# An interleaved long convolution and MLP on one core: another order for the first three quarters of its operations

## The chip, the cores and the metric

The kernel runs on one core of one Trainium2 chip. The metric is the device time of one execution in microseconds (us); the median of three executions stands for a kernel. A profile shows one more execution.

The core has five engines, each of which takes its own instructions strictly in order: TensorE (PE in the profile; its weight loads are PEld), VectorE (DVE), ScalarE (ACT), GpSimd (POOL) and SyncE (SP). They wait for each other and for transfers by semaphores. Here SyncE issues nearly all transfers (DMA), GpSimd a few gathers.

## The reference

With a sequence of 2048 rows and 640 channels, all in float32, the reference computes

```python
x = q
for _ in range(2):
    x = x + A(layernorm(x), k, v)
    x = x + relu(layernorm(x) @ w1) @ w2          # 640 -> 1728 -> 640

def A(q, k, v):                                   # H3 layer
    k_shift = causal_depthwise_conv(k, shift_k)   # 4 taps
    kv = k_shift * v
    y = long_causal_conv(kv, ssm_k) + kv * ssm_D  # 2048 taps per channel, by FFT
    return q * y
```

The convolution doesn't depend on `x`: only its gate, the last product, does. Its result is the same in both rounds, so the kernel computes it once and uses it twice.

## The kernel before, in words

**Tiles.** The sequence is cut into 8 chunks of 256 rows; a chunk has two halves of 128 rows, one per partition. Names carry the chunk: `x2_0` is half 0 of chunk 2's activations, `xT2_1` the transposed, layer-normalised input of chunk 2's second MLP.

**The MLP.** `prep` computes the statistics, normalises (`xnB`), splits the result into two float16 halves (the high one by ScalarE, L1154; the low one by VectorE, L1155) and has SyncE transpose both, for each half chunk, by DMA (L1182) into `xT`: `xT2_1_00` is the high part, `xT2_1_01` the low one. `main` then multiplies: the first product `mm1` (L1319 and L1321 for the first block of columns, where the low part is read last; L1331, L1332, L1334 for the others) into PSUM tiles `h`, of which ScalarE takes the relu's high half `hh` (L1470) and VectorE the rest `hl` (L1471), and the second product `mm2` (L1303, L1304, L1306) into `o` and `oc`, in half blocks of two groups of columns. So `hl10_0` is the low half of the first block of MLP number 10.

**The convolution.** It runs over pairs of channel tiles ("units", named by chunk and tile, `4_2`). `transform` loads `kt` and `vt` (keys and values), `hf` and `hr` (the long filter), applies the four taps (`acc`, on ScalarE L479 and L529 and on VectorE L536 and L553), forms the spectra of the filter (`pg`, L585, with the constants `cG` and `cX`) and, over a transpose `pt` and its eviction `sh` (L651), those of the input (`pr`, L656, with the constant `cM`), evicts them to `gt` and `at` (L670), mirrors them by a GpSimd gather (`at<-at`, L626), and stores them in DRAM (`A`, `G`). `products` loads `Ax` and `Gx` back (L748), multiplies (`pd`, L761), adds up (`pacc`, L766), and transforms back into `u`, `pq` and `ys`, which is stored as `Y`. Each chunk goes through both rounds before the next ones do (a layernorm needs only its own row), so the units of later chunks run beside the MLPs of earlier ones, and after the last unit the MLPs of the last chunks go on alone.

**The order.** The functions above don't issue instructions; they record 4073 operations, with what each reads and writes, in a `Plan`. `table` decodes a constant, `ORDER`, into a permutation of them, and `issue` goes through it once. So `ORDER` alone sets the order of the instructions on every engine's queue, and also in what order buffers of a ring are handed out. Which wait belongs to an instruction follows from what it reads and writes, not from `ORDER`.

```python
    def table(self):
        return [self.ops[k] for k in np.frombuffer(base64.b85decode(ORDER), "<u2")]

    def issue(self):
        for o in self.table():
```

**The start.** TensorE has nothing to multiply yet and runs throwaway matmuls (`spin`, L1579, L1599). ScalarE runs a throwaway square root (`warm`, L1575). SyncE's queue sends the first loads. `kt_0` and `kt_4` share a buffer.

Of the kernel before, what the change touches and what calls it, by code (L numbers as in the profile page):

```python
# [26 lines left out]
C = 256
# [38 lines left out]
    "ssOA2umH3GjsVgC(*U>t*8q<IHvzQ(?f}&QIRV%JCIKh`DglrHECJa7E&=cW+W;^DG66IJI{~%;ya3by)&Sf9+5kNPw*Wr@-2glR"
    "-T>kNJ^?@hHUT&RIsp&?y#NvcNdZd%5djkc;{fac?Epam-vCVk^8ge9PXS5+OaZ<CLIFboL;)2676IS@<^UZ5?*QQd7XkbLMFIT)"
    "{s2({=KxayzW^8kMgdg;=l~f3M*&v>ApsfzSpfk7NCAZb=>Q`ETLB^gZ2@iph5>K^BmwaN@&Jbci2;fMivdmnT>%0CZvg`V1OagY"
    "{{VUc_5h3lUjcFf9szR!Pytc_Q~`DYhyh^%bOBZYSOHoATmfDIcmZGmV*!l;j{#HwjsbT8djVnrkpO)Gd;w$uzX5px<p6#GWdXne"
    "W&wWzkO9E~X91A`k^%GpfC0h*XaQ*f!vVzs#sMG!!~tpnlL3JNlmV3ix&X@o%mK#%_W;NNmjRXmnE}lKf&yy+m;r+U^#IWU>j2UL"  # L70
    "$pHWX$^p{>&H;o0@&TLyngP@Sp8=f#fCBRY^Z^9{g94xd^#P#)_5t_+q5=2;`2n5*_W{oV&;j`XqXDG>qyf7C`T&~&hysBEi2|nq"
    "`T?c^`v9o{r~&)|{Q-sos{#7~2LXoyssYyl+5y-BtO2b7Yylhr*#T7m+X2-99|5HTgaWSt0s`Ryg#xDniUP0!t^w8o-T?*y2m#*#"
    "u>rFIvH=MJ3jrGe-~o#Qv;lPi3IVkN3;_cIi~`&N-2tfr9|NWWf&sSywgKV+xB=w>;{mGz=K<sajslMY*aGMQxdG_`+5)-(lmhAj"
    "4FTo>>jAp~jRNce{sFuJl>)s1tOB|Mw*rs?z5x#bkplk#00IF5?E#kpr~>W*?*Rk?3IdV>m;&$tmI4I=z5)mW@c||RCjuw}ssfV&"
    "1_HSPy8<NwxB{61DFO`wDgp@t2Lj{(ECQSY4gw1T4+5P66aw4=y#l}jtpY6qE&>h#ngTBZt^%F{paKj66#^Clp8~J~5dsndFan_h"
# [5 lines left out]
    "UjkzSV+08UegZ-RU;<?VWCAJ!)&eU7rvx1Xe*$O(W&$h&EdvSz3j;#~Hv}&OFarz&4FfI%L<2<wF#`?*X#{HoJp?}lX97k8K?F|("
    "Q3OH+M+15UXaYb4G6ORMLj*_z9s_IyNdry;s06A6Py{psN&`y+4+CieH3LrrL<B_yPy<E;QUp^3R0CB5Y63O`M+A5THv>2WZ3IXJ"
    "O$1B>ZUj*SRs&4~QUg;1S_4!BIRjk-Nd!s+Is<?NJOfSyR|IbaR|9?o5CeMzSOZxDRRnMZaRgQbUIR-6fdoDSOayWSs{~sEg9L;G"
    "Tmy0fYXW2gd<1g@qy%9DJp*C`Wdm3QUju&xU<0NEK?6GjSp-@Hdjf(4W&?BtV*_~vX9H>jbp);ih6Hv5g#>5=TLfzZTm-NLhXj!X"
    "Km%O_#RRDYhy-i{_ym0fbpw(Fi3F4cb_2%*l?3_(iUi06Z3908lLU_hUIeiOuLNlWZUc7%iv)NBj0Bbh8U=R*%>=9jkObQU`~-~z"
    "js$N5a077ztps@kaszq;djrk{nFPxO%mmN`d;@(0{RDvn&jfP=#srrHngoIag9EYz(*&CYgafk#wgi|2v;@=ye*^ynU<A<wegl95"
    "00p%KbOW3OhXaTM`2>vv(gcYEodk*lw*<HZ{se^skOPqeh69cRo&*C0j{~^`mjlTJp9Iwex&(^@)&%<m0R@x;y9B%hl>?Roj04vM"
    "k^{;Fz68Al*aX}J*#wva-UOWklLK%Co&(<m-~^xqcm=-%zyz5C;RKrlc?FsS+60^f0tKi8p97!+!35m|;soOa<OIS51O=%B!vv}W"
    "1qI~<b_E;-<^*vCA_T4j1_fUPp#ygXuLH0H=LDhz2L<Q^#02UDqXnx2dIft0q64f0+XM&&?gXO)r3HQkas{yiqyu~f2?ewRwF3(U"
    "=>)9<3I(MD>jduveFf|UrUP>Yrv(fJx&ylde+7UAwgU|XrvtJByaT-hvjevS4h6si4+Y!<@C4lh-UHtQs0H8y;sb#N5C!oB@&pkD"  # L90
    "xC3+rss+OX69uaU%>{J@?F9A&qy@wSf(5|?xdW~R!UOXJ;{)UasRa@Rz5~AluLZ{g$OGjA<^vQ3u?5Nlg9XV0=L6^itOe-<#RJR*"
    "^aO_mgayU}rUexRtp)1?&;zms76t4Bi3QOE%LC2>&jZo}%md8>iUo)T7zNY=)dh<M(*xB5?F01$)&tiAvjvO=jRlSc?*r}w@B{G!"
    "@&k_r7X|eLum!aRp#+fy*aP+h)CJiCk_FlWkOhSWBLwpUBm|QMwgvP9B?Kk}v<0^X;RE{v)&=(i_yhR^h6Nb~Cj==3{{;aC`~&I("
    "C<H15D+JdC`U5NkEd-SXxCH?O{{#I40tA!={sS%q00fx@0|W#F0|waz2LuELF9Zk#2?Uk}Fa!k#1q2EN1_lNM3<L)T2nGuT4g{A4"
    "8wC#p5Cjnf*ag}J+XdkTng#a+9R)H3AO+6_5(Etd69h8^9tE2P&IKU_m<1mN6$BRq3I@;xA_XG_7z7yvoCOpFBn2e}Ck43$8U!>1"
    "odqZbo&_}ox&<i(76cmv90V!_Jp~H}D+SR79RwZ(F$4_;J_Qa2p9KsCECtd99|Rx-KLtPqK?Onuy9K=kyahuAL<L0!E(g;E5e7yD"
    "Nd+whN(B=JM+Ha)O$ELMzXeML;sqfDE(HPxPX$l~F9k3KOa%Z2zy+WMq6Jk2+yzbr2?pH-F$GZtU<XnKV+S$?SOq2p4+g;nRt4S#"
    "-vz=2C<apnR0UZD5C&HTTm>x$GX-4*Uj<$TH3eD)U<JbkIR)bdVFfe=F9$XSWd+0q6b5AnXa~gw<ON#=Y6lVq#sy*pV+A(_W(8*j"
    "<pt&i6$Uy5#|1bAWCdvj=LKj5$OXv-Y6WWrYy~w3$^|<G=mqNq>;>rs>IL8h?FBXmW(V&DNe1o(76$YMJOyn983t|zN(S%+%LNw("
    "Fb5b0PX;juZw2uM^#wQw@&!u<Oa}G^8U||z^94`_O$IjyIR_gCDF*iiZ3i+3ItNY$90nZ*9tI%>X$SZPI|n=mZwHD8Q3fgoRR(hh"  # L100
    "QwCH9GY29DLI)oPQU*N-WC!^L`UPPJJ_kPsAO=JSRtEb8LkE)wGzTjNE(R|KBL-UrTn1tXiw9>1BnEH?k_ROQSq4`ICI&?ZMhCqI"
    "S_YH{SO%2`Uj|?XYzO=WM+YYcECxsiFa~Z1KnF1fT?R=9N(V9qEe4hcUIt7Dmj^QjH3l~ZbO%cZO$TuYatC1sP6vz!=Lb&*jR!Uc"
    "Vg@({WCm3SV+K$MIR-igI|i5sJO*V3b_Zw%X$DaTQU_`VQwKc;W(H>lnFqiJbq78McL%};YX)ovZw7D%K?gquZ3dqQRtJs;kOwpd"
    "ZU$Eecn5h0R0qWepa-`G!3RJFK?Xwxdj~=Wbq2==xCW00dI!D-d<R4Z$Ol*laRzb*a|V3}Mh002eg}32ng^Q)MFz$PbOxLUfCixl"
    "kq4p&e+NeffCoqhcLsO{c?Nn0zXziS!w2vO?+0E7#0P-}$_LB`$p?D|d<K06S_jYv8VIBZTL&Eoeg=XDg9d~Kr3Zfoxd!nEh6d;d"
# [1628 lines left out]
```

## Time and profile before

| | |
|---|---|
| three executions | 838.88, 840.49, 842.19 us; median 840.49 |
| the profiled execution | 842.58 us; span on the core 840.8 us, granted clock 0.999 |
| TensorE busy | 831.8 us of the span (99%) |
| VectorE busy | 777.0 us (92%) |
| ScalarE busy | 604.2 us (72%) |
| GpSimd busy | 45.8 us (5%) |
| transfers | 182.37 MB, 217 GB/s over the span |

The span runs from the first to the last instruction; the execution's own time is 1.8 us longer. A row of the timeline gives start, duration, engine, line, operation, what is written and read, and in brackets how long the engine was idle before it and what it waited for. A row of the waits gives the total, the number and the longest. "DMA to landing" is the time from the issue of a transfer to its arrival. In a row of windows the engines' busy times stand in the order PE, PEld, DVE, ACT, POOL, with the granted clock, the share of DMA and GB/s at the end.

### The profile page before, as it was taken

To read this page: it belongs to the slowest core of one execution; us is meant where nothing else is said; L and a number is where in the kernel's file an instruction comes from. 1 tells how busy PE (TensorE), PEld (TensorE's weight loads), DVE (VectorE), ACT (ScalarE), POOL (GpSimd) and SP (SyncE) were. 2 spreads that over 40 slices of the span, in tenths; PEclk is the share of its full clock that TensorE was granted. 3 is DMA by queue.
4 is the path that set the end of the run, shared out by engine and by line. 5 is a ranking of instruction groups with operands and counts; after the bars stand their busy time and mean duration, and the time that the engine had idled before them with its cause. 6 is when DMAs were issued, how large, how long until landed. Compare 5 with 4: busy or idle time off the path is not lost.

```text
span 840.8 us, 20661 instructions
## 1 busy us (share of the span) xinstructions
PE 831.8 (99%) x8135; PEld 660.3 (79%) x8135; DVE 777.0 (92%) x1404; ACT 604.2 (72%) x1505; POOL 45.8 (5%) x58
## 2 busy tenths in 40 slices
...
GB/s 276 378 278 256 241 322 180 324 259 238 310 253 226 219 220 265 228 297 211 191 314 182 264 237 179 256 215 249 276 301 268 102 241 126 79 87 4 58 34 32
DMA packets 138435, 182.37 MB, mean 217 GB/s; under 512 B 53857, under 2 KB 95713, under 8 KB 138338
## 3 DMA queue, kind: packets, MB, share of 16 engines
...
q14 instruction: 34, 0.28, 0.1%
q10 hardware_dynamic: 144, 0.10, 0.0%
...
## 4 chain that ended last, share of the span: by engine, by line
PE 90%; DMA 4%; DVE 3%; issue 2%; ACT 1%; POOL 0%; POOLq 0%; DVEq 0%; ACTq 0%
PE o L1249 9%; PE h L1331 9%; PE h L1332 9%; PE h L1334 9%; PE o L1304 8%; PE o L1303 8%; PE o L1306 7%; PE h L1319 4%; PE oc L1303 2%; DMA at<-at 2%; PE oc L1304 2%; PE h L1321 2%; PE pg L585 2%; PE oc L1306 2%; PE hs L1364 2%; PE h L1364 2%
## 5 line engine op out<-in xcount | busy, mean ns | idle before, releaser
L1331 PE MATMUL h<-xT,w 128*128 128x256 f16 (+1 forms) x1000 | 229.1, 249 | 0.6 <-DVE hh L1479 0.4
L1334 PE MATMUL h<-xT,w 128*128 128x256 f16 (+1 forms) x1000 | 229.1, 249 | 0.0
L1332 PE MATMUL h<-xT,w 128*128 128x256 f16 (+1 forms) x1000 | 229.1, 249 | 0.0
L1304 PE MATMUL o<-w,hh 128*128 128x512 f16 x336 | 127.3, 379 | 0.0
L1303 PE MATMUL o<-w,hh 128*128 128x512 f16 x336 | 127.3, 379 | 0.0
L766 DVE TENSOR_TENSOR pacc<-pacc,pd 128x1536 f32<-128x1536 f32 (+1 forms) x75 | 123.2, 1642 | 0.5
L1332 PEld LDWEIGHTS <-w 128*128 128x128 f16 x1100 | 107.6, 98 | 14.4 <-issue 1.0
L1331 PEld LDWEIGHTS <-w 128*128 128x128 f16 x1100 | 107.5, 98 | 13.9
L1334 PEld LDWEIGHTS <-w 128*128 128x128 f16 x1000 | 97.8, 98 | 6.3
L1304 PEld LDWEIGHTS <-hh 128*128 128x128 f16 x672 | 65.7, 98 | 27.1
L1303 PEld LDWEIGHTS <-hh 128*128 128x128 f16 x672 | 65.7, 98 | 26.9 <-ACT hh L1470 0.2
L1470 ACT ACTIVATE hh<-h 128x512 f16<-128x512 f32 (+1 forms) x97 | 46.9, 484 | 50.5 <-PE h L1334 19.6
L1306 PE MATMUL o<-w,hl 128*128 128x512 f16 x208 | 78.8, 379 | 0.0
L761 DVE TENSOR_TENSOR pd<-Ax,Gx 128x768 f32<-128x768 f32 x83 | 77.6, 948 | 0.4 <-DMA Gx<-G 0.2
L1304 PE MATMUL oc<-w,hh 128*128 128x128 f16 x336 | 73.6, 219 | 0.0
L1303 PE MATMUL oc<-w,hh 128*128 128x128 f16 x336 | 73.6, 219 | 0.0
L1306 PEld LDWEIGHTS <-hl 128*128 128x128 f16 x416 | 40.7, 98 | 25.5 <-DVE hl L1471 0.9
L1319 PE MATMUL h<-xT,w 128*128 128x256 f16 (+1 forms) x400 | 57.7, 251 | 1.6 <-DMA xT<-xh 1.6
L479 ACT ACTIVATE tp<-kt,shs 128x256 f32<-128x256 f32 (+1 forms) x78 | 43.9, 574 | 6.4 <-DVE acc L553 3.7
L1306 PE MATMUL oc<-w,hl 128*128 128x128 f16 x208 | 45.6, 219 | 0.7 <-DVE hl L1471 0.7
L761 DVE TENSOR_TENSOR pd<-at,Gx 128x768 f32<-128x768 f32 x46 | 43.0, 950 | 2.9 <-DMA at<-at 1.8
L501 POOL DMA_DIRECT2D gs<-hr x20 | 19.1, 953 | 420.1 <-PE h L1334 228.6
...
## 6 DMA issues: line engine op xcount, KB each, us to landing
Ax<-A SPq DMA_DIRECT2D x89, 384.0 KB, 5.0
Gx<-G SPq DMA_DIRECT2D x89, 384.0 KB, 4.9
...
```

What stands on the lines that cost most here:

```text
L479: ACT.activation(o[:, i : i + m], kview(i, m, j), AF.Copy, scale=shs[:, t, j : j + 1])
L761: ew(f"mac{j % POOLMOD}", 768, lambda e, x=dst[i], av=av, gv=gv: e.tensor_mul(x.t, av(), gv()), [ax, gx], [dst[i]], pr_)
L766: dve(768 * (hi - lo), lambda lo=lo, hi=hi, pd=pd: DVE.tensor_add(acc[:, lo:hi], acc[:, lo:hi], pd[:, lo:hi]), [*sums[lo:hi], *dst[lo:hi]] ...
L1249: PE.matmul(b[:, c : c + w], x, y[:, z : z + w], start=done[i] == 1, stop=end, skip_group_check=fin)
L1303: PE.matmul(z, hh[:, c], wh[:, d], start=(j == JS[0] and i == 0 and (h == 0 or s == S[0])), stop=False)
L1304: PE.matmul(z, hh[:, c], wl[:, d], start=False, stop=end and tail)
L1306: PE.matmul(z, hl[:, c], wh[:, d], start=False, stop=end)
L1319: PE.matmul(p[:, z], wh, xv(t, x), start=b and x == 0, stop=e and x == 1)
L1331: PE.matmul(p[:, z], wh, xv(t, 0), start=b, stop=False)
L1332: PE.matmul(p[:, z], wh, xv(t, 1), start=False, stop=tail and e)
L1334: PE.matmul(p[:, z], wl, xv(t, 0), start=False, stop=e)
L1470: act(2 * R, lambda pv_=pv_, hh=hh: ACT.activation(hh.t, pv_(), AF.Relu), [src], [hh], URGENT)
```

## The change: another permutation

The constant `ORDER` is replaced by another of the same length; all other lines are the same, and so are the 4073 operations. The first 3000 or so are moved: by 4 places in the median, by 19 or less in nine of ten, by 255 at most. The last thousand stand where they stood. The rows of base 85 tell a reader nothing; two of each:

```diff
@@ -58,81 +58,81 @@
 RPE, RBW, RLAT = 0.0, 330e3, 1.9
 ROOM = {}
 ORDER = (
-    "0{{d71po#B2LK2F2>=QJ3jhoN4FC=R4*(DV5dabZ695zd6#y0h7XTOl82}mp8vq;t9RMBx9{?Z#RsbOYA^;-*BmgA<SpWb4R{#M3"
-    "CIBY@C;$QgTL4i2T>xGHTmX^)QUECcDgY}0EC4M4E&wk8FaR+CG5|9GGypXKHUKvOH~={SIsiKWJODiaJ^()eKmb7iLI6VmL;ytq"
...
+    "0{{d71po#B2LK2F2>=QJ3jhoN4FC=R4*(DV5dabZ695zd6#y0h7XTOl82}mp8vq;t9RMBx9{?Z#Apjx(BLE}-B>*M>Cjck_DF7+}"
+    "D*!A2EdVY6F90wAF#s|EGXOLIH2^jMHvl*QIRH8UI{-WYJpfVwQ2<#000031J^)$(RsdT7T>w`ATmV=A0svqDVE|qLUjSwRX8>pb"
...
+    "&I^VMKMJJ_stbt=s|!F1*$Y7mLJF)4)C-3T6AGvc+6xs5tqau)Lkgw~-3vqt77D2g6beQP+Y8<ct_v9oS_{|<iVH^y8VcYGNDAQ#"
+    "rwgwOunS2F-wTTijSJ)p;tLxJ912PbOA4|J9STee9tw;L<qJ&;u?w>cAPOQ1P6|&7PzoUm9}2V!=L_fy+zaLlCkjytC<;^x;|sP6"
```

What moved can be seen in the queues of the engines. A row has the line, the operation, what is written and what is read; the last number of a name only counts buffers and differs between the two.

**The start, ScalarE.** `acc0_0` is the first tap of unit `0_0`, `pg` and `pt` are PSUM tiles of TensorE. Before:

```order
L1575 ACT_TABLE_LOAD
L1575 ACTIVATE warm_102<-epst_88 128x1
L529 ACTIVATE acc0_0_201<-kt0_0_184,shs_101 128x256
L479 ACTIVATE acc0_2_258<-kt0_2_208,shs_101 128x256 x2
L588 ACTIVATE gt0_0_286<-pg00_0_252 128x2x2x128
L588 ACTIVATE gt0_0_286<-pg10_0_270 128x2x2x128
L651 ACTIVATE sh0_0_305<-pt0_0_294 128x512
L479 ACTIVATE acc0_4_324<-kt0_4_292,shs_101 128x256
```

Now:

```order
L529 ACT_TABLE_LOAD
L529 ACTIVATE acc0_0_226<-kt0_0_224,shs_101 128x256
L1575 ACT_TABLE_LOAD
L1575 ACTIVATE warm_102<-epst_88 128x1
L588 ACTIVATE gt0_0_243<-pg00_0_238 128x2x2x128
L479 ACTIVATE acc0_2_272<-kt0_2_254,shs_101 128x256 x2
L588 ACTIVATE gt0_0_243<-pg10_0_245 128x2x2x128
L479 ACTIVATE acc0_4_316<-kt0_4_300,shs_101 128x256
L651 ACTIVATE sh0_0_326<-pt0_0_303 128x512
```

The tap of `kt0_0` stands ahead of `warm`, there are two loads of a table in place of one, and `acc0_4` stands ahead of `sh0_0`. On SyncE's queue `cX`, `cG`, `hf0_0`, `shs` and `dDs` now come ahead of `kt0_0`, and `cM`, which was sent ahead of `kt0_4`, is sent behind it. TensorE's queue has 60 spins ahead of its first `pg` in place of 72, and two more matmuls of `pg` ahead of its first `pr`.

**The eviction of `at4_2`, ScalarE**, on its way to the GpSimd gather that the products of unit `4_2` read; these products stand ahead of `hl10_0` on VectorE. Before:

```order
L1150 ACTIVATE x2_0_2907<-x2_0_2907,means_96 128x640
L404 ACTIVATE hlu04_1_6240<-u04_1_6090,zu4_1_6123 128x512
L397 ACTIVATE za4_3_6215<-pna4_3_6214,tiny_97 128x1
L1470 ACTIVATE hh9_4_6260<-h9_4_6173 128x512
L394 ACTIVATE png4_3_6262,zg4_3_6263<-gs04_3_6071 128x512
L394 ACTIVATE png4_3_6262,zg4_3_6263<-gs14_3_6074 128x512
L670 ACTIVATE at4_2_6118<-pr14_2_6207,za4_2_5621 128x2x256
L670 ACTIVATE at4_2_6118<-pr04_2_6082,za4_2_5621 128x2x256
```

Now:

```order
L404 ACTIVATE hlu14_1_6212<-u14_1_6099,zu4_1_6084 128x512
L404 ACTIVATE hlu04_1_6214<-u04_1_6081,zu4_1_6084 128x512
L670 ACTIVATE at4_2_6150<-pr14_2_6152,za4_2_5624 128x2x256
L1492 ACTIVATE hh9_6_6113<-tl_86 64x256
L670 ACTIVATE at4_2_6150<-pr04_2_6137,za4_2_5624 128x2x256
L479 ACTIVATE tp14_4_6222<-kt4_4_6097,shs_101 128x512
L397 ACTIVATE za4_3_6177<-pna4_3_6176,tiny_97 128x1
L1470 ACTIVATE hh9_4_6264<-h9_4_6159 128x512
L394 ACTIVATE png4_3_6272,zg4_3_6273<-gs04_3_6071 128x512
```

`za4_3`, `hh9_4` and the two sums `png4_3` stand behind the last eviction of `at4_2`, and so does the update of `x2_0`. On VectorE's queue `hl10_0` has the same instructions ahead of it as before, and one add of `acc4_4` (L553) more.

**The low half of `xh2_1_01`, VectorE** (L1155), which the transpose into `xT2_1_01` reads; TensorE reads this tile in the first block of MLP number 10. Before, it stood five rows behind its pair `xh2_1_00`:

```order
L1155 TENSOR_TENSOR xh2_1_00_6078<-xnB2_1_00_6076,xh2_1_00_6078 128x640
L761 TENSOR_TENSOR pd4_2_6_6170<-Ax4_2_3_2_6153,Gx4_2_2_2_6129 128x768
L1493 SCALAR_TENSOR_TENSOR hh9_6_6080<-tl_86,hh9_6_6080 64x256
L761 TENSOR_TENSOR pd4_2_4_6159<-Ax4_2_2_2_6019,Gx4_2_3_2_5896 128x768
L761 TENSOR_TENSOR pd4_2_6_6170<-Ax4_2_3_2_6153,Gx4_2_1_2_6205 128x768
L1155 TENSOR_TENSOR xh2_1_01_6236<-xnB2_1_01_6105,xh2_1_01_6236 128x640
L405 SCALAR_TENSOR_TENSOR hlu14_1_6218<-u14_1_6120,zu4_1_6123,hlu14_1_6218 128x512
```

Now it stands 21 rows behind it:

```order
L405 SCALAR_TENSOR_TENSOR hlu14_1_6212<-u14_1_6099,zu4_1_6084,hlu14_1_6212 128x512
L1471 SCALAR_TENSOR_TENSOR hl9_4_6267<-h9_4_6159,hh9_4_6264 128x512
L761 TENSOR_TENSOR pd4_2_6_6261<-Ax4_2_3_2_6111,Gx4_2_1_2_6216 128x768
L766 TENSOR_TENSOR pacc4_2_6144<-pacc4_2_6144,pd4_2_4_6196 128x1536
L398 RECIPROCAL za4_3_6177<-za4_3_6177 128x1
L398 RECIPROCAL zg4_3_6273<-zg4_3_6273 128x1
L405 SCALAR_TENSOR_TENSOR hlu04_1_6214<-u04_1_6081,zu4_1_6084,hlu04_1_6214 128x512
L766 TENSOR_TENSOR pacc4_2_6144<-pacc4_2_6144,pd4_2_6_6261 128x1536
L1471 SCALAR_TENSOR_TENSOR hl9_5_6346<-h9_5_6225,hh9_5_6328 128x512
L405 SCALAR_TENSOR_TENSOR hlg04_3_6322<-gs04_3_6071,zg4_3_6273,hlg04_3_6322 128x512
L1155 TENSOR_TENSOR xh2_1_01_6146<-xnB2_1_01_6129,xh2_1_01_6146 128x640
```

Ten instructions that stood behind it stand ahead of it. On SyncE's queue its transpose has the transposes of the other three quarters, a store of G and a load of `vt4_4` ahead of it, and behind it loads of A and G that were sent before it. On TensorE's queue the same matmuls stand ahead of the first read of `xT2_1_01`.

Three more places: on VectorE four instructions of other tiles moved ahead of the low half of `xh1_0_00`, while on TensorE eleven matmuls moved ahead of the first read of its transpose. On TensorE two half blocks of `mm2` moved ahead of the first read of `xT3_1`, on VectorE six instructions ahead of the low half of `xh3_1_01`. And after these SyncE's queue has the store of `x2_0` and the load of `x4_0` ahead of loads of A and G that stood ahead of them.

More of the change, by code (lines that the diff above doesn't have):

```diff
@@ L66 @@
[L66 to L75, printed above, removed]
@@ L81 @@
[L81 to L90, printed above, removed]
@@ L91 @@
[L91 to L105, printed above, removed]
@@ new lines @@
+    "HUT^VKLOML+5px75CJ{`KmpzW5&`1?H~~5VK><ktO94Uw5djkc6ah*BOaVgy>;T^Y76HBh-~dDc?EpmqMgiskO##0EM*$T97Xje_"
+    "NC8g)7y;-2=KvW2Apso$g#l3k=>Ss!8UZ2!@&Jbc`~V{XZ2^V>i2;iN{Q&*|ZUF%SZvk-u0s#X71OZh6Bms&6Z~<2V{{V;qasl=L"
+    "dI4DhP61E>QUO~5Q~_N9^Z;`K9syqgb^(k5RsmrFjRAK7bOCz-d;wztjsaK!S^-=Ej{$uFcma6<egXFYkO7eaf&#w*e*u62UIAbM"
+    "VgY0UWdXne!2!Yn!vT^3y8vbZX8~vd!~v55#R0|vfdR(>>i~lRgaOL|lmW~EX#r{hl>x{B^#GRv(E)=3mI2KHm;spq&H;b|YXQ;$"
+    "<p7!i(*dOdoB^Eyp8?4M@&TR!^8xe$^#RlY_y7O_paG!)$^rNR`2qF;&jF$V&;bPjqXDG>_W}6;n*pQ&`T(Z^rU4rPx&Vj*r~&!`"
@@ new lines @@
+    "`v9o{`~lYis{#E1`vC_5gaWJqrve56+5y`E9|45|*a3zDi2~ID*#QUvtpTb5hXQN?iUO$ut^oo9ivq6!90863umO((0|MRw;Q`_S"
+    "i~@B5-vQtOu>l|fjRNBVr~<M92>}ZMvjMdM3IYBB3<2Z;{{hwklmeClv;nsP=K<US-2ssRkOH;=fdc3Okpj5^4FTl=<^i_?l>+Gj"
+    "mjb#0f&sVzy8){LyaDO~y#eb1>;b+3?E&rq4gt9W00NQ%9|O7q1Ok`>tO5Z73IYWJrULH)2m-qT@B!EY@d23v<Nyr<B?2Y_4gx0v"
+    "ssh>qlLBl42?7rR1_BEL2LdPpDFWOA6au~iDgrD5-U6HgngSI9tpW@JodPWa4+0hfE&>+<t^yGPy#l-f5(1tAumZmVu>vmw8UmmK"
+    "Q~)pnp8^m9zyiSnRRF>QuL3aw5d#wfp#qx%G6FLK!vfg?xB?RcvH}|d!~z%sq5`u5wF0yPH3G!~+XBY|83M=x$^sk$#scjE$pSV4"
@@ new lines @@
+    "G6ORMJp^Y0Nds~MN&|ZY4+DAxP6Iy#Km;@c9s{TZXaZ>hPy|Z@LIgwvPXkf}Q3O;2RRc8xHUmQhY646HO#?*)Py<l|Mg%tlQv|96"
+    "Z3GYlM+9yJI0IG#Is;MzQv*l@cmz!ZR|8H2R|H7}c?5t2fdpCuYXUw4N(5K~IRkG5s{}j)R0LfEO9WX1RRnPaRs?<oas*oga0FZf"
+    "UIV5CWCJ||g9Kp%gamU0e*}UAqy%CEUjtwRbOcNUSOjAObp$~Jd<0npWdp7RXahR~Km%q2X#;iyeFRzrX9I==djf|9Tm*##8U?8Y"
+    "Y6DvYumo!Z#{^vjbpv+<Yy+$Wkpz+i#RQZDlLYt#UId5)l>~_diUe*0b^~_<uLPC^cmt0FZv%M)Z3A!vkOa#Fiv;=vj0DXDu>{Bj"
+    "tpv^l`~-0WU<7*ud;^UHjs%$mngntKdINz2a|3+?f&={omjr_YvILt1e*??}gafk#KLh^+fCHQawgiU*&;*DBv;=+wm;?X?wFJ=w"
```

90 lines of the change are left out of this document (54 added, 36 removed).

## Prediction

> **What bounds the kernel now.** I read the page's busy table first, then the waits of TensorE (PE), then the windows of the stage in which most of its waits lie.
>
> ```profile
> PE 831.8 (99%) x8135; PEld 660.3 (79%) x8135; DVE 777.0 (92%) x1404; ACT 604.2 (72%) x1505; POOL 45.8 (5%) x58
> PE spin L1579 <- POOL heps L362: 2.0, 1, 2.0
> PE h L1319 <- DMA xT<-xh: 1.6, 2, 1.0
> PE oc L1306 <- DVE hl L1471: 0.7, 1, 0.7
> PE h L1331 <- DVE hh L1479: 0.4, 1, 0.4
> PE h L1331 <- DVE tl L1490: 0.2, 1, 0.2
> 415.00:460.00 45.00, 45.00 (x388) 34.21 (x386) 44.74 (x69) 34.19 (x84) 6.52 (x7) 1.00 0.87 241
> ```
>
> TensorE is busy for 831.8 of 840.8 us at a granted clock of 1.00. Of the 9.0 us that are left, 2.0 lie before its first matmul, some 4 behind its last one, and 2.9 in five waits: two for transposed activations (1.6), one for the low half `hl` of a relu output (0.7) and two of 0.4 and 0.2. No reordering of these instructions can win more than the 2.9 us (0.35%) between the first matmul and the last, and half a per cent, 4.2 us, is about what a measurement of this kernel can tell from no change. The windows show the danger: from 415 to 460 us VectorE (DVE) is busy for 44.74 of 45, so there it is as full as TensorE, and a wait that a new order gives to VectorE is handed on.
>
> The three largest of the five waits, which I take for the three of the change, have these rows:
>
> ```profile
> 156.14 0.44 PE L1319 MATMUL h<-xT,w 128*128 128x128 f16 x5 [0.66 <-DMA xT<-xh]
> 366.65 1.83 DVE L761 TENSOR_TENSOR pd<-at,Gx 128x768 f32<-128x768 f32 x2 [1.83 <-DMA at<-at]
> 375.36 0.23 PE L1306 MATMUL oc<-w,hl 128*128 128x128 f16 x1 [0.74 <-DVE hl L1471]
> 412.85 0.27 PE L1319 MATMUL h<-xT,w 128*128 128x256 f16 x1 [0.99 <-DMA xT<-xh]
> ```
>
> Together 0.66 + 0.74 + 0.99 = 2.39 us.
>
> **The wait at 156 us: -0.66.** The late transfer is the transpose of the low half, which is issued behind the VectorE instruction that makes that half (L1155). In the change four VectorE instructions of other tiles stand ahead of that one that stood behind it before (an add of the taps, a relu rest, one `ys`, one `hla`).
>
> ```profile
> 147.32 0.81 DVE L1155 TENSOR_TENSOR xh<-xnB,xh 128x640 f16<-128x640 f32 x1
> 148.16 0.75 DVE L405 SCALAR_TENSOR_TENSOR hla<-pt,za,hla 128x512 f16<-128x512 f32 x1
> ...
> 149.54 0.28 DVE L1493 SCALAR_TENSOR_TENSOR hh<-hb,hh 64x128 f16<-64x128 f32 x1
> ...
> 150.20 0.75 DVE L845 TENSOR_TENSOR ys<-pq,qs 128x256 f32<-128x256 f32 x2
> 156.96 0.22 PE L1304 MATMUL oc<-w,hh 128*128 128x128 f16 x1
> 157.01 0.38 PE L1303 MATMUL o<-w,hh 128*128 128x512 f16 x1
> 157.23 0.38 PE L1304 MATMUL o<-w,hh 128*128 128x512 f16 x1
> DMA to landing us min/median/max: 2.6/4.1/6.6
> ```
>
> Three of them ran from 148.16 to 149.82, the fourth is half of the 0.75: 1.7 + 0.4 = 2.1 us, so the half is ready at 148.1 + 2.1 = 150.2, or at 151.0 if the relu rest comes no sooner than at 149.54 and two of the others follow it. TensorE has eleven more matmuls ahead of its first read of the tile, 1.6 us at 0.055 for each of the five narrow ones and 0.215 for each of the five wide ones (from start to start in the rows below) and 0.27 for the last; it asks at 156.14 - 0.66 + 1.6 = 157.1. With the longest landing of this window, 6.6, the transfer is there at 156.8 (157.6 at worst). I take the wait as gone; the worst leaves 0.5 of it.
>
> **The wait at 375 us: -0.74.** `hl10_0` has the same VectorE work ahead of it as before and 0.69 more (one add of the taps). What sets its time is the idle stretch of 1.83 that ends at 366.65, a wait for a gather by GpSimd (`at<-at`) that follows ScalarE's (ACT's) last eviction of `at4_2`.
>
> ```profile
> 351.13 0.82 ACT L1150 ACTIVATE x<-x,means 128x640 f32<-128x640 f32 x1
> ...
> 352.47 0.24 ACT L397 ACTIVATE za<-pna,tiny 128x1 f32<-128x1 f32 x1
> ...
> 354.46 1.25 ACT L670 ACTIVATE at<-pr,za 128x512 f32<-128x512 f32 x2
> 356.10 1.20 POOL L626 DMA_DIRECT2D at<-at  x1 [8.65 <-ACT at L670]
> ```
>
> In the change five ScalarE instructions stand behind the eviction that stood ahead of it: the one at 351.13 (0.82) and the four from 352.47 to 354.46 (2.0), 2.8 us. If the eviction comes 2 us sooner and the gather takes as long as before (10.5, from 356.10 to 366.65), the idle 1.83 goes, `hl10_0` comes 1.83 - 0.69 = 1.14 sooner, and the 0.74 goes too. If the gather isn't sooner, the wait becomes 0.74 + 0.69 = 1.43; that is a rival below.
>
> **The wait at 412.85: -0.99.** Two more half blocks of the second product (`mm2`: 12 narrow matmuls at 0.055 and 12 wide at 0.215) stand ahead of the first read of `xT3_1`: 3.2 us. The late transfer was issued at 407.52; in the change ScalarE has three more instructions ahead of its source (some 2.1 us), SyncE's (SP's) queue has another transpose and a load ahead of it, and 409.6 (2.1 later) plus the 2.6 to 5.2 of the rows below lies around the 415.1 at which TensorE now asks. Gone, with little to spare.
>
> ```profile
> 407.52 2.59 SPq L1182 DMA_TRANSPOSE xT<-xh  x1
> 411.08 0.81 DVE L1155 TENSOR_TENSOR xh<-xnB,xh 128x640 f16<-128x640 f32 x1
> 415.69 0.68 DVE L1471 SCALAR_TENSOR_TENSOR hl<-h,hh 128x512 f16<-128x512 f32 x1
> 421.19 0.71 PE L1319 MATMUL h<-xT,w 128*128 128x256 f16 x5
> DMA to landing us min/median/max: 2.6/4.1/5.2
> ```
>
> Its low half is read at 421.19, without a wait. The six VectorE instructions that ran behind the one that makes it (411.08), up to 415.69, now stand ahead of it: ready at 415.8, on the chip at 419.9 (4.1) or 421.0 (5.2). TensorE asks at 421.19 - 0.74 - 0.99 + 0.65 (six more matmuls) = 420.1. New wait 0 to 0.9; I take 0, by the median landing.
>
> **A new wait at 368 us: +2.3.** Here the low half of `xh2_1_01` was made at 354.98; in the change ten VectorE instructions that came behind it stand ahead.
>
> ```profile
> 354.98 0.82 DVE L1155 TENSOR_TENSOR xh<-xnB,xh 128x640 f16<-128x640 f32 x1
> 355.71 0.74 DVE L405 SCALAR_TENSOR_TENSOR hlu<-u,zu,hlu 128x512 f16<-128x512 f32 x1
> 361.97 0.47 DVE L847 SCALAR_TENSOR_TENSOR ys<-pq,zu,qs 128x256 f32<-128x256 f32 x1
> 368.34 0.71 PE L1319 MATMUL h<-xT,w 128*128 128x256 f16 x5
> DMA to landing us min/median/max: 6.3/9.1/10.0
> DMA to landing us min/median/max: 2.6/3.8/10.0
> ```
>
> From 355.71 to 361.97 ran eight of them, and the other two (`za`, `hlg`) add 0.7: 7.0 us, so the half is ready at 355.8 + 7.0 = 362.8 and its transpose can't be issued sooner. TensorE has the same matmuls ahead and asks at 368.3. The three transposes of this stage took 6.3 to 10.0 to land (first of the two rows; the second is that of all 61): with the stage's median of 9.1 the tile is there at 372.0 and TensorE waits 3.7; with its shortest, 6.3, it waits 0.9; with the median of all, 3.8, nothing. For the long end speaks that it is the same transfer in the same stage; for the short one that SyncE, which issues in order, stands at this transpose and has sent little for some us ahead of it. I take the middle of 0.9 and 3.7. The ends are 0 and 3.7.
>
> **The start: +0.7.**
>
> ```profile
> 0.74 1.28 ACT L1575 ACT_TABLE_LOAD   x1 [0.74 <-PEq L1719]
> 2.17 0.43 SPq L462 DMA_DIRECT2D kt<-in_kT  x1
> 5.49 0.51 ACT L529 ACTIVATE acc<-kt,shs 128x256 f32<-128x256 f32 x1 [3.26 <-DMA kt<-in_kT]
> kt<-in_kT SPq DMA_DIRECT2D x1, 262.0 KB, 3.7
> cM<-in_cM SPq DMA_DIRECT2D x1, 384.0 KB, 5.5
> 14.70 1.08 PE L656 MATMUL pr<-sh,cM 128*128 128x256 f32 x4
> ```
>
> Before, ScalarE loaded its table while nothing else was there to do, and `cM` was sent ahead of `kt_4`, which waits for VectorE's last read of `kt_0` in the same buffer. Now a load of 1.28 stands ahead of the first tap of `kt_0`, a second one behind it, `kt_0` itself is sixth and seventh in SyncE's queue, and `cM` is behind `kt_4`. The seventh issue starts near 3.9 in place of 2.17 (the fourth before), so the tap that started at 5.49 ends near 5.5 + 1.7 + 1.28 + 0.5 = 9.0, VectorE's last read, 1.8 behind it as before, near 10.8, and `cM` leaves at 11.2. With its 5.5 it lands at 16.7; TensorE, with two more matmuls of 0.27 ahead, asks at 14.70 + 0.5 = 15.2: a wait of 1.5. With the 3.7 of a smaller load of this stage it lands at 14.9 and nothing waits. Fewer transfers are out at 11 us than before, so I take the middle.
>
> On a switch of tables the Trainium skill ("ScalarE: Activation LUTs", section "What ACT_TABLE_LOAD costs") says that a load of about 1283 ns is followed by a drain of about 1380. The load agrees with the 1.28 of the row; the drain isn't seen there, since `warm` starts at 2.04. By the page the tap would come 1.38 later and, as `cM` hangs on it, the start would cost 2.1 in place of 0.7.
>
> **From 415 to 460: +0.9.** SyncE's queue there has the store of `x2_0` and the load of `x4_0` ahead of the A and G spectra that stood ahead of them. Two issues of some 0.4 make 0.9; VectorE, which reads those spectra, idles 0.26 in 45 us, so there is no slack to hide it. The other end is one wait as long as VectorE's at 366.65, 1.8; the low end is nothing.
>
> **The sum.** -0.66 - 0.74 - 0.99 + 0 + 2.3 + 0.7 + 0.9 = +1.5 us. On the profiled execution (842.58, span 840.8) that is 844.1; it stood 2.1 above the median of the runs (840.49), on which the same sum gives **842.0**.
>
> **The rivals.**
> - *Nothing takes the waits' place*: -2.39, 838.1 (837.5 if all five go). For it speaks that all new waits are lateness of transfers that mostly land in 4 us; against it the 9.1 of the stage at 368.
> - *The low half's transposes hold SyncE's queue*: slower. At 362.8 the queue stands at that transpose, and the loads of A and G behind it leave after it. With 9.1 to land the wait is 3.7, the one at 420 comes to 0.9, and VectorE's waits to 1.8: -2.39 + 0.7 + 3.7 + 0.9 + 1.8 = +4.7, 845.2. It decides from a landing of some 9 us at 362.8. For it speaks the row 6.3/9.1/10.0; against it that lateness at 368 gives VectorE time to catch up.
> - *The gather isn't sooner*, so the change leaves the wait at 375, now 1.43: with the tile at 368 on time, -0.66 - 0.99 + 0.69 + 0.7 + 0.9 = +0.6, 841.1. Against it speak the five ScalarE rows that leave its way.
>
> **How the numbers follow.** Forecast 0.50, no replacement 0.17, held queue 0.23, gather 0.10. Faster by over 0.5% (under 836.3) is out of reach of the waits alone and stands only for an unlike run: 0.04. Slower by over 0.5% (over 844.7) takes 0.18 of the held queue and 0.10 of the forecast's upper side: 0.28. The rest, 0.68, is no change. All new costs at their upper ends (1.5 + 0.5 + 3.7 + 0.9 + 1.8) less 2.39 give 846.5, all at zero 838.1; the range is 838.0 to 846.5.
>
> **What would show it.** Right: in TensorE's waits the three rows are gone, a wait for `xT<-xh` near 368 of 1 to 4 us and one of up to 1.5 near 15 for `cM` or `sh` stand there, and VectorE's wait for `at<-at` near 366 is gone. Wrong: no wait at 368 (then the landing followed the emptier queue), a wait at 375 (then the gather was as late), or waits of TensorE between 415 and 460 that sum to over 1.8. A sum of waits about that of before with another time would show that the runs differ by something no wait tells.

## The result: 0.6 to 0.8 per cent slower

Five executions of the changed kernel took 845.47 to 849.09 us, median **845.78**; the kernel before, beside it, 839.75 (838.88 to 842.19). The ratio is 1.008, its 95% interval 1.0053 to 1.0106. A second comparison (below) gave 846.4 against 841.2, a ratio of 1.006 (1.0048 to 1.0072), +5.2 us. The time lies inside the range of the prediction, but the likeliest case, no change, didn't come.

The profiled execution of the change took 845.47 us (span 843.7, clock 1.00), only 2.9 more than that of before (842.58). The one is the fastest of the change's five, the other lies above all the times of before just given, so a step is judged below by several traces.

The busy times of the changed kernel and TensorE's three largest waits behind the start (total us, number, longest):

```profile
PE 832.8 (99%) x8135; PEld 660.6 (78%) x8135; DVE 775.6 (92%) x1404; ACT 604.5 (72%) x1506; POOL 45.7 (5%) x58
PE pnu L396 <- ACT pnu L394: 1.4, 2, 1.0
PE pq L384 <- DVE hlu L405: 1.2, 1, 1.2
PE h L1331 <- DVE hl L1479: 1.0, 1, 1.0
```

The three aimed at are gone, but for 0.46 of the one at 375 us, and others stand in their place: 4.87 us behind the start in place of 2.96. The new ones name VectorE and ScalarE, but for 0.35 us on a load of weights at 33 us. The row of the third, at 348 us (the second lies at 456), and the rows of VectorE where it waits longest between 340 and 460 us:

```profile
347.85 0.27 PE L1331 MATMUL h<-xT,w 128*128 128x256 f16 x1 [0.98 <-DVE hl L1479]
346.50 0.96 DVE L761 TENSOR_TENSOR pd<-Ax,gt 128x768 f32<-128x768 f32 x1 [2.36 <-DMA gt<-gt]
382.74 0.96 DVE L761 TENSOR_TENSOR pacc<-Ax,gt 128x768 f32<-128x768 f32 x1 [1.49 <-issue]
449.58 0.96 DVE L761 TENSOR_TENSOR pd<-Ax,gt 128x768 f32<-128x768 f32 x1 [1.09 <-DMA gt<-gt]
```

VectorE waits 2.36 + 1.49 + 1.09 = 4.9 us for three mirror gathers by GpSimd (`gt<-gt`, L626; `issue` in the second row stands for no wait that the profile names, but its operand `gt4_3` is another such gather, issued at 375.45 and landed 7.2 later, at 382.65, just ahead of the read). They belong to the units 4_2, 4_3 and 6_0. One us behind the first, TensorE waits for the `hl` that VectorE made late. This reads as a chain: gather, VectorE, TensorE, in the stages where VectorE has nothing to spare. The experiments put parts of it to the test.

### The profile page after: what moved, and what is told of

Its sections match the earlier page's. It is cut to its first block, busy times and chain, and to the rows that moved or that the text cites. A ratio compares the mean times of both kernels' runs of the same rounds, so it can differ in the third digit from the quotient of the medians.

```text
span 843.7 us, 20679 instructions
## 1 busy us (share of the span) xinstructions
PE 832.8 (99%) x8135; PEld 660.6 (78%) x8135; DVE 775.6 (92%) x1404; ACT 604.5 (72%) x1506; POOL 45.7 (5%) x58
## 3 DMA queue, kind: packets, MB, share of 16 engines
q8 instruction: 63, 1.03, 0.5%
## 4 chain that ended last, share of the span: by engine, by line
PE 70%; DVE 14%; DMA 9%; issue 4%; ACT 1%; SPq 1%; POOL 0%; POOLq 0%; DVEq 0%; ACTq 0%
PE o L1249 9%; PE h L1331 7%; PE h L1334 7%; PE h L1332 7%; PE o L1304 6%; PE o L1303 6%; PE o L1306 5%; DVE pd L761 3%; PE h L1319 3%; DVE pacc L766 3%; DMA gt<-gt 2%; PE h L1364 2%; PE hs L1364 2%; DMA gs<-hr 2%; DMA ws<-in_w 2%
```

## The experiments

Every kernel is another permutation of the same 4073 operations and computes all of it. In the diffs a row is an instruction of one queue, without buffer numbers; `...` stands for rows left out. All medians and ratios are against runs of the kernel before on the same chip.

### The two kernels again

No edit.

> The kernel before, word for word, for a second profile and further times. Theory J (the waits aimed at were those of one execution): the profiled execution of before took 842.58 us, its five timed ones have a median of 839.75, so some 2.8 us of what its trace shows isn't there in most executions. J expects 839 to 840 us, and of the three rows at 156 us (0.66), 375 us (0.74) and 413 us (0.99) at most one over 0.3 us; the sum of TensorE's waits behind the start falls from 2.95 to under 1.5 us. Theory F (the waits are fixed by the order): all three rows come back within 0.3 us, sum 2.5 to 3.4 us, whatever the time.

Measured: 841.21 us, ratio 0.9999 (0.999 to 1.0008), profiled 840.57, span 838.8; 839 to 840 had been expected. All its waits of TensorE behind the start:

```profile
PE h L1319 <- DMA xT<-xl: 0.6, 1, 0.6
PE h L1319 <- DMA xT<-xh: 0.5, 1, 0.5
PE h L1331 <- DVE hh L1479: 0.4, 1, 0.4
```

One wait for `xh` is left, the one at 156 us. Those at 375 and 412.85 are not there, and not in the traces of any of the kernels below that keep the old order at these places either; the one at 156 is there in all of them that keep the old order at 156, with 0.50 to 0.65. So of the 2.39 us that the change aims at, 1.73 were the accident of one execution, and some 0.6 were to be had.

> The changed kernel, word for word, for a second profile and further times. In its first trace TensorE waits 4.87 us behind the start, the largest at 347.85 us (0.98, VectorE hl L1479), 455.79 us (1.19, VectorE hlu L405) and 583.72 us (1.03, ScalarE pnu L394), all for engines and none for a transfer. If they follow from the new order (theory N) all three come back within 0.4 us and the time is 845 to 846. If they too are one execution's (theory J for both kernels), at least two of the three are gone or at other places, while the time stays at 845 to 849.

Measured: 846.4 us, ratio 1.006 (1.0048 to 1.0072), span 844.7. TensorE's waits behind the start sum to 5.03. The longest, and VectorE's wait ahead of it:

```profile
PE h L1331 <- DVE hl L1479: 2.4, 1, 2.4
347.58 0.96 DVE L761 TENSOR_TENSOR pd<-Ax,gt 128x768 f32<-128x768 f32 x1 [3.77 <-DMA gt<-gt]
```

The waits at 375 and 584 (1.03 in the first trace) are not there; both traces show the one behind the gather of unit 4_2 (0.98 and 2.40) and one for `hlu` near 456 (1.19 and 0.59). So neither theory holds as a whole: two of the three waits follow from the new order, by sizes that differ from execution to execution.

### Which half: the new order up to 318 us, or from there on

In the one kernel the first 1808 places are those of the change (up to there both orders hold the same set of operations; the expectations below say 1807) and the rest stands as before; the other is the reverse. It cuts at 318 us of the trace.

```diff
+ places 0 to 1807 of the new table
  places 1808 to 4072 of the old table
```

> The new order for its first 1807 places (up to about 318 us, the two orders hold the same operations up to there), then the order of before. Theory L (the loss lies behind this place, in the waits at 348, 456 and 584 us): 839 to 840 us, no slower than before; by the first traces the new order is even 0.4 us ahead at 318 us. Theory S (the loss is made at the start and carried along: second table load, cM behind kt_4, and 0.66 saved at 156 us): 841.5 to 843, and 4 us of the 6 are in this kernel.

> The order of before for the first 1807 places (up to about 318 us), then the new one. Theory L: 844.5 to 846.5 us, the whole loss of 6 us, with TensorE's waits near 348, 456 and 584 us as in the changed kernel. Theory S: 841 to 842.5 us. If the two halves each show less than half of the loss, the loss needs both (a lead or lateness of one engine that the first half hands to the second).

> The new order up to about 318 us and the old one behind it, a second time, since in the first it stood 0.6 us below the kernel before (ratio 0.9995, 0.9986 to 1.0004) and its trace had no wait of TensorE behind the start at all. If the early half of the change is a gain: 0.3 to 1.0 us below the kernel before again, with TensorE's waits under 0.8 us in sum. If that was chance: within 0.3 us of it, with waits of 1 to 2 us.

Measured: early half 840.58 us, ratio 0.9995 (0.9986 to 1.0004), and again, later, 840.25, 0.9994 (0.9983 to 1.0005); late half 846.23, 1.0063 (1.0048 to 1.0078). In the first trace of the early half TensorE's list of waits has one row (line numbers here are 5 lower):

```profile
PE spin L1574 <- POOL heps L357: 1.9, 1, 1.9
```

So the start and everything up to 318 us costs nothing that can be told from zero, both times with a small gain inside the interval, as the 0.6 at 156 would give; the whole loss lies behind 318 us. The second trace of the early half has 0.97 at 12.91 (for `pt`'s operand `sd`), 0.20 and 0.44, so these, too, differ from execution to execution: the small gain that had been expected came again, but not with waits under 0.8.

### The load beside the gather of unit 4_2

On SyncE's queue, the change sends a load of 384 KB for VectorE's products, which stood behind the transpose `xT2_1_00`, ahead of it. The rows of SyncE and GpSimd there, and the landing of that gather, in the change and then in the second trace of before:

```profile
338.09 0.46 SPq L748 DMA_DIRECT2D Gx<-G  x1
338.60 0.42 SPq L748 DMA_DIRECT2D Ax<-A  x1
338.15 1.22 POOL L626 DMA_DIRECT2D gt<-gt  x1 [3.09 <-ACT gt L629]
DMA to landing us min/median/max: 8.3/8.3/8.3
```

```profile
338.99 0.46 SPq L748 DMA_DIRECT2D Gx<-G  x1
342.75 1.20 SPq L1182 DMA_TRANSPOSE xT<-xh  x1
344.00 0.57 SPq L748 DMA_DIRECT2D Ax<-A  x1
339.05 1.22 POOL L626 DMA_DIRECT2D gt<-gt  x1 [2.77 <-ACT gt L629]
DMA to landing us min/median/max: 6.0/6.0/6.0
345.10 1.83 DVE L761 TENSOR_TENSOR pacc<-Ax,gt 128x768 f32<-128x768 f32 x2 [0.18 <-DMA gt<-gt]
```

In both the gather is issued 0.06 us behind the start of a load of `Gx`. In the change a second load goes out 0.5 later, and the gather lands 8.3 after its issue in place of 6.0. First, the row is put back in the change:

```diff
-L748 DMA Ax4_2_3_2
 L1182 DMA_TRANSPOSE xT2_1_00
+L748 DMA Ax4_2_3_2
```

> The changed order with one row of SyncE's queue moved back: the load of Ax4_2_3_2 (384 KB) behind the transpose into xT2_1_00 instead of ahead of it, as it stood before. In both traces of the changed kernel the mirroring gather of gt4_2, issued about 0.5 us ahead of that load, lands after 8.3 and 9.7 us and VectorE waits 2.4 and 3.8 us for it; in three traces with the old order there it lands after 6.0 to 6.3 and VectorE waits 0.2 to 0.6. Theory G (the load, sent at the same moment, slows the gather): it lands after 6.5 us or less, VectorE's wait falls below 0.7, TensorE's wait near 348 us (0.98 and 2.40, hl L1479) is gone, and the time is 1 to 2.4 us below the changed kernel: 844.0 to 845.4 us where that has 846.4. Rival R (VectorE is simply short of time from 340 us on, and the gather's wait only shows it): the wait for the gather may shrink but TensorE's come back within 50 us, and the time stays within 0.5 us of 846.4.

Measured: 843.88 us, ratio 1.0041 (1.0025 to 1.0058), some 2 us less than the change; the gather's landing and VectorE's wait:

```profile
DMA to landing us min/median/max: 6.2/6.2/6.2
343.40 0.96 DVE L761 TENSOR_TENSOR pd<-Ax,gt 128x768 f32<-128x768 f32 x1 [0.25 <-DMA gt<-gt]
```

TensorE's wait at 348 is gone. This trace is of the fastest of twelve executions; they spread from 842.04 to 847.03, and four of them, over 846, are no faster than the change. Then the same row alone was moved ahead in the kernel before:

```diff
+L748 DMA Ax4_2_3_2
 L1182 DMA_TRANSPOSE xT2_1_00
-L748 DMA Ax4_2_3_2
```

> The order before with one row moved: the load of Ax4_2_3_2 ahead of the transpose into xT2_1_00, as the change has it. Theory G: the gather of gt4_2 lands after 7.5 to 9.7 us in place of 6.0 to 6.1, VectorE waits about 2 us for it and TensorE 0.5 to 1.5 near 348 us, and the time is 1.5 to 2.7 us above the kernel before (this row and the store's together cost 4.2). Rival T (the pair costs what it costs only together): under 0.8 us.

Measured: 842.79 us, ratio 1.0019 (1.0008 to 1.0029), some +1.6 us. The gather's landing, VectorE's wait for it and TensorE's for VectorE:

```profile
DMA to landing us min/median/max: 8.3/8.3/8.3
347.69 1.83 DVE L761 TENSOR_TENSOR pacc<-Ax,gt 128x768 f32<-128x768 f32 x2 [2.48 <-DMA gt<-gt]
PE h L1331 <- DVE hl L1479: 1.1, 1, 1.1
```

One row, put back or put in, turns the landing from about 6 to over 8 us, VectorE's wait from 0.2 to 2.4, and the time by 1.6 to 2. Of the loss this part is shown from both sides; of the two, only the run on the old order has an interval well clear of nothing (0.7 to 2.4 us).

### The stores from 415 to 460 us

SyncE's queue in the change has the store of `x2_0`, the load of `x4_0` and, behind that, the store of `x2_1`; the loads overwrite buffers that the stores read, so each waits for the store ahead. Before, the store of `x2_1` stood ahead of both; it is this store that moved, and the load of `x4_0` went ahead of one load of `Gx`, while the store of `x2_0`, which the rows of the change name, kept its place. The two loads went out 4.4 us apart, while in the second trace of before one row at 424.02 held both, and ScalarE waits 3.47 us for the second one:

```profile
427.99 0.33 SPq L1082 DMA_DIRECT2D x<-in_q  x1
432.38 0.33 SPq L1082 DMA_DIRECT2D x<-in_q  x1
437.14 0.74 ACT L1084 ACTIVATE jq<-x 128x640 f32<-128x640 f32 x1 [3.47 <-DMA x<-in_q]
```

My theory was that this delays ScalarE and so the gather of unit 6_0. The store was put ahead again in the change:

```diff
 L1566 DMA out<-x2_0
+L1566 DMA out<-x2_1
 L748 DMA Gx4_4_1_4
 L1082 DMA x4_0
-L1566 DMA out<-x2_1
+L1082 DMA x4_1
 L748 DMA Gx4_4_0_4
 L748 DMA Ax6_0_0_0
-L1082 DMA x4_1
```

> The changed order with two rows of SyncE's queue moved: the store of x2_1 goes ahead of the load of x4_0 (which takes the buffer of x2_0 and waits for its store to land), and the load of x4_1 directly behind that of x4_0. In the changed order SyncE stands at x4_0's load for one store's landing and then at x4_1's for the next (428.0 and 432.4 us, where the order before has both at 424.0), ScalarE waits 1.5 and 3.5 us for the two loads, the gather of gt6_0 is issued 2.8 us later than before, VectorE waits 0.4 to 2.2 us for it and TensorE 0.6 to 1.5 at 456 us (pq, hlu L405). Theory G2 (this chain): x4_1's load 2 to 4 us earlier, ScalarE's two waits together under 2 us, TensorE's wait at 456 us gone; 1.0 to 1.8 us below the changed kernel, 844.6 to 845.4 us. Rival R: within 0.5 us of 846.4.

Measured: 845.9 us, ratio 1.0058 (1.0039 to 1.0077). No gain:

```profile
434.17 0.74 ACT L1084 ACTIVATE jq<-x 128x640 f32<-128x640 f32 x1 [0.42 <-DMA x<-in_q]
443.06 0.63 ACT L629 ACTIVATE gt<-gt 128x512 f32<-128x512 f32 x1 [2.09 <-DVE gt L623]
451.59 0.96 DVE L761 TENSOR_TENSOR pd<-Ax,gt 128x768 f32<-128x768 f32 x1 [2.69 <-DMA gt<-gt]
```

ScalarE's wait for the load fell from 3.47 to 0.42, but the copy ahead of the gather (L629) then waited 2.09 for VectorE, and VectorE's wait for the gather was 2.69. The trace is of the slowest of six executions (848.03), but the median of the six is about that of the change. In it the gather landed 7.5 after its issue, against 5.9 and 5.2 in the two traces of the change. The theory falls: that wait of ScalarE is real, and the time didn't hang on it. Undoing the load and the stores together, with that copy (L629) of unit 4_3 moved ahead of five other instructions on ScalarE:

```diff
+L629 ACTIVATE gt4_3
 jkA3_1_00, hh10_0, jkA3_1_01, za4_3, stdA3_1_0
-L629 ACTIVATE gt4_3
```

> Both of the moves above in one kernel, and a third: ScalarE's last step for gt4_3 (L629) goes back ahead of five instructions of the layernorm and of hh10_0, so that its gather is issued some 1.5 us earlier; VectorE waits 1.5 to 1.7 us for it at 383 us in the changed order and not at all before. These are the three gathers for which VectorE waits about 5 us between 340 and 450 us. Theory G: 841.5 to 843.5 us, most of the 5.2 us between the two kernels gone, with no TensorE wait over 0.5 us between 318 and 500 us. Rival R: over 845.

Measured: 845.69 us, ratio 1.0051 (1.0032 to 1.007); 841.5 to 843.5 had been expected. The gather of unit 4_3:

```profile
371.54 1.19 POOL L626 DMA_DIRECT2D gt<-gt  x1 [19.21 <-ACT gt L629]
DMA to landing us min/median/max: 9.0/9.0/9.0
380.60 0.96 DVE L761 TENSOR_TENSOR pacc<-Ax,gt 128x768 f32<-128x768 f32 x1 [1.33 <-issue]
```

It took 9.0 us to land and VectorE waited all the same: issuing a gather earlier was no way to have it earlier here. TensorE's wait at 456 stood at 1.47, where none over 0.5 had been expected. This gather is slow in all traces of the late half of the change: 7.2 to 7.9 us in the six others, against 5.3 to 6.4 in the seven that have the old order there, in which VectorE doesn't wait for it. What lengthens it was not tried.

### Two of the rows in the old order

The load ahead (as above), and the store of `x2_1` behind the load of `x4_0`, together on the kernel before:

```diff
-L1566 DMA out<-x2_1
 L1566 DMA out<-x2_0
 ...
 L1082 DMA x4_0
+L1566 DMA out<-x2_1
```

> The order before with two rows of SyncE's queue moved to where the change has them: the load of Ax4_2_3_2 ahead of the transpose into xT2_1_00, and the store of x2_1 behind the load of x4_0. All else is the order before. Theory G: gt4_2's gather lands after 7.5 to 9.7 us in place of 6.0, x4_1's load leaves some 4 us later, TensorE waits appear near 347 and 455 us, and the time is 842.5 to 844.5 us where the kernel before has 841.2. Rival S (the old order has slack for this, and the loss needs the other moves too): 841.2 within 0.6 us.

> The order before with the other row moved: the store of x2_1 behind the load of x4_0, as the change has it. Theory Q (SyncE stands at x4_0's load until x2_0's store has landed and at x4_1's until x2_1's has; the loads behind are sent together, some 6 us later, and the gather of gt6_0 lands among them, after 8.8 us in the run with both rows): x4_1 leaves near 430 us in place of 424.8, gt6_0's gather lands after more than 8 us, TensorE waits 1 to 2 us near 455 and 467 us, and the time is 1.5 to 2.7 us above the kernel before. Rival T: under 0.8 us.

Measured: both rows 845.04 us, ratio 1.0049 (1.0031 to 1.0068), +4.2; the store alone 844.55, 1.0036 (1.0023 to 1.005), some +3.0, which with the 1.6 of the load alone adds up to about both. Both rows and the store alone cost somewhat more than had been expected (842.5 to 844.5 us, and 1.5 to 2.7 above). The trace of the store alone: loads, the gather of unit 6_0 and VectorE's wait for it, and the window from 446 to 448 us (engines' busy times, clock, DMA share, GB/s):

```profile
425.28 0.34 SPq L1082 DMA_DIRECT2D x<-in_q  x1
430.67 0.34 SPq L1082 DMA_DIRECT2D x<-in_q  x1
441.89 1.20 POOL L626 DMA_DIRECT2D gt<-gt  x1 [1.17 <-ACT varA L1046]
DMA to landing us min/median/max: 8.5/8.5/8.5
450.43 0.96 DVE L761 TENSOR_TENSOR pacc<-Ax,gt 128x768 f32<-128x768 f32 x1 [2.05 <-issue]
446.00:448.00 2.00, 2.00 (x19) 1.33 (x17) 2.00 (x4) 2.00 (x6) 0.45 (x1) 1.00 1.03 325
```

The same window and gather in the second trace of before:

```profile
424.02 1.54 SPq L1082 DMA_DIRECT2D x<-in_q  x2
440.89 1.20 POOL L626 DMA_DIRECT2D gt<-gt  x1 [2.49 <-ACT varA L1046]
DMA to landing us min/median/max: 6.8/6.8/6.8
446.00:448.00 2.00, 2.00 (x20) 1.42 (x19) 1.62 (x3) 1.33 (x4) 0.91 (x1) 1.00 0.62 99
```

The loads go out 5.4 us apart in place of one behind the other. The gather goes out no later than in other traces of the old order (439.75 to 443.25), but it takes longer: 8.5 us, and 8.8 with both rows, against 6.3 to 7.3 in the five traces that have the store in its old place. In both kernels the DMA engines are full from 442 to 446 us (shares of 0.99 to 1.10); from 446 to 448 they still are with the store behind (1.03, 325 GB/s), while in the second trace of before they are at 0.62 and 99 and the gather lands at 447.7. So the store does cost in the old order, and putting it back in the new order (above) brings nothing: there something else makes the same wait.

### The reads of the gather of unit 6_0

In the change VectorE reads that gather ahead of two products of `Gx` that stood ahead of it before (2 x 0.9 us). Put back behind them, with the load of unit 4_2 put back too:

```diff
-L761 pd6_0_2<-Ax6_0_1,gt6_0
 L761 pd6_0_2<-Ax6_0_1,Gx6_0_5
 ...
-L761 pacc6_0<-Ax6_0_0,gt6_0
 L761 pd6_0_4<-Ax6_0_2,Gx6_0_5
+L761 pacc6_0<-Ax6_0_0,gt6_0
+L761 pd6_0_2<-Ax6_0_1,gt6_0
```

> The changed order with the load of Ax4_2_3_2 back behind the transpose, as in the run that took 2.2 us off, and two rows of VectorE's queue moved: the two reads of the mirrored gt6_0 that the change put first (pd6_0_2 and pacc6_0) go behind the two products with Gx6_0_5 (0.95 us each), as they stood before. Moving the stores of x2 made the loads earlier and the time no better, so the theory is now: at 450 us VectorE asks for gt6_0 some 1.8 us too early, since these two products no longer stand ahead of it. It expects VectorE's wait for that gather (0.4 to 2.7 us in five traces) under 0.8, TensorE's wait for hlu L405 near 453 us (0.6 to 1.5) under 0.5, and 0.6 to 1.5 us less than the kernel with the load alone: 1.5 to 2.4 us above the kernel before. Rival: VectorE is late there for all its work, the wait for the gather goes but TensorE's stays within 0.3 us of what it was, and the time stays 3 us above the kernel before.

Measured: 842.41 us, ratio 1.0019 (1.0007 to 1.0031). TensorE's waits sum to 2.01 behind the start, none over 0.45; the longest of them, the longest wait of VectorE that is left for a gather, and that gather's landing, here and then in the second trace of before:

```profile
PE pr L656 <- DMA cM<-in_cM: 0.4, 1, 0.4
381.03 0.96 DVE L761 TENSOR_TENSOR pacc<-Ax,gt 128x768 f32<-128x768 f32 x1 [2.00 <-issue]
DMA to landing us min/median/max: 7.7/7.7/7.7
```

```profile
DMA to landing us min/median/max: 5.3/5.3/5.3
```

The waits at 348 and 456 are gone. By the ratios the change costs 0.60%, with the load back 0.41%, with both back 0.19%: of 5.0 us, the load is 1.6, the order of the reads 1.9 and the rest 1.6. The first two are each known to within about 1.7 us and the rest to within 1.0, since the three ratios have intervals of 0.12 to 0.17% to each side. So the reads are only just clear of nothing, and they weren't moved in the old order by themselves; for them speaks that VectorE's wait for this gather and TensorE's at 456 went together. VectorE's wait for the gather of unit 4_3, 2.00, stands beside the rest; it wasn't undone by itself.

## Why the prediction was right in its range and wrong in its likeliest case

- **"Together 0.66 + 0.74 + 0.99 = 2.39 us" is the first step that failed.** The sum took three waits of one trace as the kernel's own. The second trace of before, and those that keep its order there, have none at 375 and 412.85. Only the 0.66 recurs (0.50 to 0.65), and that step was right: in neither trace of the change is there a wait at 156. The waits were read from an execution that lay above all five timed ones of the kernel before.
- **The wait at 375.** The step to the gather was right: ScalarE's eviction and the gather of `at4_2` came sooner (issued at 352.93), and VectorE no longer waits. But it didn't take "as long as before (10.5)": it landed in 4.1, in both traces of the change. And the wait at 375 doesn't hang on it alone: four more traces with the old order there have waits of VectorE for this gather, of 0.39 to 1.01, and none of TensorE at 375, while the first trace of the change has 0.46 at 375 behind this row without a wait:

```profile
366.04 1.82 DVE L761 TENSOR_TENSOR pd<-at,Gx 128x768 f32<-128x768 f32 x2
```

- **"A new wait at 368 us: +2.3" measured 0, because the landing was carried over from the trace.** The late half was made as worked out, 1.3 later even, and its transpose went out at 364.10, which the first row shows, with SyncE's queue held from 358.2. The second row is the landing of the stage's three transposes:

```profile
364.10 1.21 SPq L1182 DMA_TRANSPOSE xT<-xh  x1
DMA to landing us min/median/max: 2.6/3.2/4.2
```

  The second trace of the change has the same 2.6, 3.2 and 4.2, where before had 6.3, 9.1 and 10.0 (and 6.7, 7.6 and 8.9 the second time). The prediction named the emptier queue as a reason for the short end, and then took the middle. Its ends are 0.1 too high by its own rows: 362.8 and 9.1 make 371.9, and TensorE asks at 368.3. The term before it, the 0 for the low half read near 420, held: neither trace of the change has that wait.
- **The load that was not on the list.** In this stage the prediction followed the transposes of `xT2_1` and the loads behind them; that a load of `Ax`, which stood behind the first of these transposes, now goes out ahead of it and beside a gather was not seen, and so put at nothing. It is 1.6 to 2 us.
- **"From 415 to 460: +0.9"**: the place is right, and TensorE's waits there, 1.41 and 1.31 in the two traces of the change, stay under the 1.8 that was named as a sign of being wrong; the mechanism is not right. Two issues of 0.4 were not the price. VectorE's reads of the gather lost the 1.8 us of products that covered it; putting the products back took off 1.9, known to within 1.7. The full VectorE that the prediction pointed at is what handed it on. That step looked at SyncE's queue alone and not at the order of VectorE's reads.
- **The start, +0.7,** holds within its bounds of 0 and 1.5: the early half as a whole comes out 0.4 to 0.5 us below before, with 0 in both intervals, and the wait for `cM` was 0 in both traces of the change and 0.45 in one other. What the prediction didn't name is a wait for `sd` at 13 us, of 0.61 to 1.14, in three of the eight traces with the new start and in none of the six with the old one. ScalarE's rows:

```profile
6.75 1.28 ACT L529 ACT_TABLE_LOAD   x1 [6.75 <-DMA kt<-in_kT]
8.05 0.51 ACT L529 ACTIVATE acc<-kt,shs 128x256 f32<-128x256 f32 x1
8.57 1.28 ACT L1575 ACT_TABLE_LOAD   x1
9.87 0.20 ACT L1575 ACTIVATE warm<-epst 128x1 f32<-128x1 f32 x1
```

  The tap ends at 8.6 for 9.0 worked out. The Trainium skill ("ScalarE: Activation LUTs", section "What ACT_TABLE_LOAD costs") has about 1283 ns for a load, as both rows have, and about 1380 for a drain with it, which neither shows: each activation starts 0.02 behind its load, and the second load 0.01 behind the end of the tap.
- **The rival of the held queue** came closest in time (845.2), for a reason that didn't come: the queue was held, as it said, but the landing of some 9 us from which it decides was 2.6 to 4.2. The rival in which nothing takes the waits' place has a gain of 2.39, of which some 0.6 was there to be had. That the time lies in the range at all is luck in the main: its upper end rests on the 3.7 at 368, the 0.9 at 420 and the 0.5 at 156, which all measured 0, and the load's 1.6 to 2 and the reads, which the prediction didn't have, came in their place.
- **"A sum of waits about that of before with another time"** came in part. The spans of the two kernels differ by 844.2 - 839.8 = 4.4 us (means of two traces each), TensorE's waits behind the start by 4.95 - 2.23 = 2.7. The other 1.7 stand in the page as longer busy time of TensorE (832.8 and 833.7 for 831.8 and 831.1, with the same 8135 matmuls). They don't lie in the last stage, which takes 78.97 us from its first matmul to its last in all four traces. What makes them was not settled.

What stays open: that 1.7, the 1.6 us that both edits leave (the gather of unit 4_3 and small waits at 412, 416 and 580 stand in that trace), and why the wait at 584 comes and goes (0.42 to 1.46 in the traces that have it). No version here beats the kernel before by more than its interval; the early half of the change, alone, was 0.05 and 0.06% under it.
